# Agent attention with a top-1 expert layer: the last batch's first expert layer as one 128-row pass and a 19-row rest in four row groups

## The chip, the cores and the metric

The kernel runs on one core of a Trainium2 chip. The metric is the device time of one execution in microseconds (us), over several executions.

## What is computed

There are four batches of 11456 tokens, 128 channels, and 49 agents. Attention goes through the agents: `sm(agents, k)` weighs the values, `sm(q, agents)` weighs the result. Each token then goes through one of eight experts.

```
a2k = sm(agents, k);  agent_v = a2k @ v            # 49 x 128 per batch
x   = sm(q, agents) @ agent_v                      # 11456 x 128 per batch
e   = argmax(x @ w_gate);  g = max softmax(x @ w_gate)
out = g * (relu(x @ w1[e]) @ w2[e])                # w1: 128 x 1024, w2: 1024 x 128
```

## The kernel before

**Most tokens of a batch choose the same expert.** The kernel picks that expert for each batch (`choose`) and runs all tokens of the batch through it. Tokens that chose another expert are recomputed afterwards in blocks of 128 and their rows overwritten by an indirect scatter (`block_layer1` to `block_out`). There are 14 such blocks: 12 early ones from the first three batches, worked on during the last batch, and 2 late ones (numbers 12 and 13) from the last batch. A loop behind everything (`tc.For_i`, line 1681) would take any blocks beyond 14; here it makes no pass.

**First layer.** Since `x` is a product with `agent_v`, the first layer is computed from the 49 softmax values directly: the weights are `agent_v @ w1[e]`, 49 rows by 1024. All values are split into an upper and a lower fp16 part. The moving tile `M` holds the softmax numerators of a chunk of 1024 tokens, turned so that agents lie on partitions: the upper part in rows 0 to 48, the lower part in rows 64 to 112, zeros between. It is made in `mm` by `ehigh` and `elow` and turned by a DMA transpose (`eturn`, line 760). The stationary `Ah` holds the upper part of the weights, twice (rows 0 to 48 and 64 to 112), and `Al` the lower part likewise. So one eighth `f` of the 1024 hidden columns takes two matmuls over the same `M`, in `layer1`:

```python
nc.tensor.matmul(ph[:, :nn], st['Ah'][:, f, :], m, start=True, stop=False)
nc.tensor.matmul(ph[:, :nn], st['Al'][:, f, :], m, start=False, stop=True)
```

**A step** is one eighth of one group of 512 tokens: `layer1` (lines 1482, 1483; 512 columns each), `upper` on ScalarE (line 1489: relu to fp16), `lower` on VectorE (line 1494: the rest to fp16), `layer2` on TensorE (line 1507: 12 matmuls of 128 columns). A batch has 22 groups of 512 tokens and one of 192, 184 steps in all. `store` and `put` scale a finished group and write it.

**What sets the order.** `Plan` is a list scheduler with one queue per engine; each piece of work has a rank (its due step), a cost, what it needs and what it takes of the pools. Its order is then issued as it stands (`tc.manual_schedule`). Beside the steps of batch b stand the keys and values of batch b+1, the queries of the next chunks, the routing, and in the last batch the leftover blocks. Constants at the top (`BB`, `LL`, `QC3` and so on) shift the ranks.

**PSUM.** Of the eight banks `psH` has four (tag `h`, the first layer), `psY` two, `psS` two (`small_ps`). A bank of `psH` is free again when `lower` has read it.

## Time and profile before

| | us |
|---|---|
| three runs, median (lowest to highest) | 1068.8 (1067.12 to 1068.86) |
| the profiled execution, its own time | 1075.88 |
| its span, first to last instruction | 1074.2 |
| mean granted TensorE clock of it | 0.98 |
| TensorE matmul (PE) busy | 1021.5 (95%) |
| VectorE (DVE) busy | 905.9 (84%) |
| ScalarE (ACT) busy | 782.8 (73%) |
| GpSimd (POOL) busy | 168.9 (16%) |

Batches follow each other without a seam. The last batch's steps run from about 780 to 1053 us of the span, the last leftover blocks to 1062, and the end of the program to 1074.2. The ends of matmuls are modelled in the profile, so the distance between the starts of two matmuls says more than their durations. L12 is line 12 of the kernel before.

### The profile page before, as it was taken

The numbers are of one execution on the slowest core, as the hardware profiler recorded it, in microseconds if no ns is written. First come the engines' busy times: TensorE is split into PE (matmuls) and PEld (weight loads), VectorE is DVE, ScalarE is ACT, GpSimd is POOL, SyncE is SP. The second block draws the span as 40 slices with busy tenths as digits, with TensorE's granted clock in tenths as the row PEclk, the third lists the DMA queues.
The fourth block names the chain that finished last, engine by engine and source line by source line (L and its number), as shares of the span: only waits on it lengthen the run. The fifth ranks groups of instructions, "written<-read, shape, count | busy, mean of one in ns | idle before, by whom it ended". The sixth has DMA issues, their size and how long they took to land. (4 is left out here: it accounts for less than half of the span.)

```text
span 1074.2 us, 34781 instructions
## 1 busy us (share of the span) xinstructions
PE 1021.5 (95%) x14163; PEld 826.1 (77%) x14163; DVE 905.9 (84%) x2106; ACT 782.8 (73%) x1513; POOL 168.9 (16%) x390
## 2 busy tenths in 40 slices
PE   7979999999999999999999999999999799899995
PEld 6848878777887878777877887777877577688885
DVE  4888999978999899978999999868899878788651
ACT  6668888765788887765888887655876587567662
POOL 1000011003101111004012010004010423311210
PEclk8969999999999999999999999999999899999998
DMA  9778989992879979861989979852574486653320
GB/s 323 197 174 203 215 210 207 213 240 77 207 194 197 225 169 207 237 172 42 239 189 192 233 177 216 203 140 78 162 173 98 119 219 158 161 189 94 113 75 17
DMA packets 304324, 186.76 MB, mean 174 GB/s; under 512 B 217385, under 2 KB 275618, under 8 KB 304160
## 3 DMA queue, kind: packets, MB, share of 16 engines
q1 hardware_dynamic: 302304, 181.20, 68.3%
q0 software_dynamic: 1568, 2.25, 1.2%
q8 instruction: 112, 1.84, 0.7%
q10 hardware_dynamic: 288, 1.05, 0.3%
q14 instruction: 52, 0.43, 0.1%
HBM read 95.56 MB, written 36.43 MB: 123 GB/s over the span
## 5 line engine op out<-in xcount | busy, mean ns | idle before, releaser
L1507 PEld LDWEIGHTS <-hh 128*128 128x128 f16 x8640 | 536.5, 99 | 139.6 <-issue 13.2
L1507 PE MATMUL py<-w2h,hh 128*128 128x128 f16 (+1 forms) x5760 | 597.4, 219 | 2.8 <-issue 1.4
L1489 ACT ACTIVATE hh<-ph 128x512 f16<-128x512 f32 (+1 forms) x736 | 415.2, 588 | 202.4 <-PE ph L1483 190.4
L1494 DVE SCALAR_TENSOR_TENSOR hh<-ph,hh 128x512 f16<-128x512 f32 (+1 forms) x736 | 470.8, 667 | 71.1 <-ACT hh L1489 66.6
L1507 PE MATMUL py<-w2l,hh 128*128 128x128 f16 (+1 forms) x2880 | 519.6, 219 | 0.4 <-issue 0.3
L1482 PE MATMUL ph<-M,Ah 128*128 128x512 f16 (+1 forms) x736 | 276.3, 375 | 13.0 <-DVE hh L1494 12.6
L1483 PE MATMUL ph<-M,Al 128*128 128x512 f16 (+1 forms) x736 | 276.2, 375 | 0.5 <-DVE Al L898 0.3
L485 DVE SCALAR_TENSOR_TENSOR hl<-ld,mul,hl 128x1024 f16<-128x1024 f32 (+1 forms) x84 | 102.9, 1231 | 7.2 <-ACT hl L480 5.8
L472 POOL TENSOR_SCALAR mul<-hb 128x1 int32<-128x1 int32 (+1 forms) x90 | 27.4, 304 | 453.3 <-DVE hb L465 427.6
L480 ACT ACTIVATE hl<-ld,mul 128x1024 f16<-128x1024 f32 (+1 forms) x84 | 91.4, 1098 | 4.7 <-DMA ld<-in_q_dram 2.4
L446 ACT ACTIVATE jk<-ld 128x1024 f16<-128x1024 f32 (+1 forms) x90 | 90.7, 1008 | 4.4 <-DMA ld<-in_k_dram 2.8
L1483 PEld LDWEIGHTS <-Al 128*128 128x128 f16 x736 | 72.0, 98 | 24.8 <-issue 18.6
L1482 PEld LDWEIGHTS <-Ah 128*128 128x128 f16 x736 | 73.0, 99 | 10.2 <-issue 3.7
L755 POOL TENSOR_TENSOR mm<-E,mm 128x392 f16<-128x392 f32 (+1 forms) x30 | 28.6, 952 | 253.9 <-DVE mm L747 140.7
L541 PE MATMUL ps_small<-agh,hT 128*128 128x49 f16 (+1 forms) x630 | 58.2, 185 | 3.2 <-DMA hT<-hl 2.5
L543 PE MATMUL ps_small<-agh,hT 128*128 128x49 f16 (+1 forms) x630 | 58.2, 185 | 1.0 <-issue 1.0
L542 PE MATMUL ps_small<-agl,hT 128*128 128x49 f16 (+1 forms) x630 | 58.2, 185 | 0.5 <-issue 0.5
L541 PEld LDWEIGHTS <-hT 128*128 128x128 f16 (+1 forms) x630 | 52.0, 97 | 6.8 <-DMA hT<-hl 3.9
L1521 ACT ACTIVATE yo<-py,cs 128x128 f32<-128x128 f32 x174 | 49.8, 373 | 7.9 <-PE py L1507 7.2
L542 PEld LDWEIGHTS <-hT 128*128 128x128 f16 (+1 forms) x630 | 50.5, 97 | 3.4 <-issue 1.2
L543 PEld LDWEIGHTS <-hT 128*128 128x128 f16 (+1 forms) x630 | 50.3, 97 | 1.3 <-issue 1.3
L737 ACT ACTIVATE E<-E,ln,div 128x392 f32<-128x392 f32 (+1 forms) x48 | 33.0, 688 | 9.2 <-DVE E L732 8.9
(296 smaller groups left out, 1154.4 us busy)
## 6 DMA issues: line engine op xcount, KB each, us to landing
ld<-in_k_dram SPq DMA_DIRECT2D x44, 512.0 KB
ld<-in_v_dram SPq DMA_DIRECT2D x44, 512.0 KB
ld<-in_q_dram SPq DMA_DIRECT2D x44, 512.0 KB
out_dram<-yo SPq DMA_DIRECT2D x88, 256.0 KB
w1e<-in_moe_w_dram SPq DMA_DIRECT2D x17, 512.0 KB
w2e<-in_moe_w_dram SPq DMA_DIRECT2D x17, 512.0 KB
exps<-E SPq DMA_DIRECT2D x44, 196.0 KB
wn<-in_moe_w_dram SPq DMA_DIRECT2D x8, 512.0 KB
```

The lines of the kernel that those rows point to most:

```text
L446: nc.scalar.activation(jk[:p, :t * D], x[:p, :t, :].rearrange("p t d -> p (t d)"), AF.Square, accum_out=ss[:p])
L480: nc.scalar.activation(hl[:p, 0, :t, :], loaded[b, src, c][:p, :t, :], AF.Copy, scale=SC[src, c][0][:p, :1])
L485: nc.vector.scalar_tensor_tensor(hl[:p, 1, :t, :], loaded[b, src, c][:p, :t, :], SC[src, c][0][:p, :1], hl[:p, 0, :t, :], op0=ALU.mult, op ...
L541: nc.tensor.matmul(o, x[:, 0, i, :p], AG["h"], start=True, stop=False)
L542: nc.tensor.matmul(o, x[:, 0, i, :p], AG["l"], start=False, stop=False)
L543: nc.tensor.matmul(o, x[:, 1, i, :p], AG["h"], start=False, stop=True)
L1482: nc.tensor.matmul(ph[:, :nn], st['Ah'][:, f, :], m, start=True, stop=False)
L1483: nc.tensor.matmul(ph[:, :nn], st['Al'][:, f, :], m, start=False, stop=True)
L1489: nc.scalar.activation(hh[:, 0, :nn], ph[:, :nn], AF.Relu)
L1494: nc.vector.scalar_tensor_tensor(hh[:, 1, :nn], ph[:, :nn], 0.0, hh[:, 0, :nn], op0=ALU.max, op1=ALU.subtract)
L1507: mm_ = lambda l, r, **k: nc.tensor.matmul(o, l, r, skip_group_check=True, **k)
L1521: nc.scalar.activation(yo[:p, i, :], py[:p, i * D:(i + 1) * D], AF.Copy, scale=cs[:, i:i + 1])
```

## The change

It changes the last batch alone, and the end.

**Packing.** `mm` and `M` now use all 128 rows: the lower part in rows 0 to 48, the upper part in rows 66 to 114, and a second copy of the upper part for agents 0 to 16 in rows 49 to 65 and for agents 17 to 29 in rows 115 to 127 (`edup`, two casts on ScalarE per chunk). `Al` holds the upper weights for the first two parts and the lower weights for the copies (`packrow`, `restrow`). So one matmul with `Al` gives everything but the lower weights of agents 30 to 48, the leftover 19 rows.

**The rest.** `rests` computes those 19 rows for four eighths at once: four matmuls of 19 rows and 512 columns, at partitions 0, 32, 64 and 96 and into four different PSUM banks, three of `psH` and one of `psS`. Its moving rows lie in `M` at partitions 96 to 114 and are copied to the other three places by three DMAs per chunk (`rest`, tile `Q`, two buffers). `Wq` has the weights; `rest_products` makes them with four small fp32 matmuls per batch, `rest_split` splits them.

**The end.** `block_out` of blocks 12 and 13 stands behind the loop in the source and leaves the plan. `keep`, the pool with their indices and values, outlives the main pools.

Beside that: the gathered rows `ex` are transposed without the copy `ex2` (line 1286); `BB` is 86 in place of 80 (the leftover blocks' rank); eleven small VectorE operations at the start make `packrow` and `restrow`. The built order of batches 0 to 2 is the same up to the preparation of the last batch's weights.

```diff
+KR = 128 - 2 * A
+UP = 96 - KR
+DUP = ((A, 0, UP - A), (UP + A, UP - A, KR))
-BB, BS, BLAG, BZ, WL, WS = 80, 8, 3, 3, 22, 10
+BB, BS, BLAG, BZ, WL, WS = 86, 8, 3, 3, 22, 10
...
+        def edup(c):
+            _, p, t = chunks[c]
+            for o, a0, a1 in DUP:
+                nc.scalar.copy(mm[c % len(mm)][:p, :t, o:o + a1 - a0], Es[c][:p, :t, a0:a1])
+
+        def rest(c):
+            _, p, t = chunks[c]
+            x = Qs[c] = mpool.tile([P, 8, P], F16, tag="Q", name="Q", bufs=MQ)
+            for r in range(3):
+                nc.sync.dma_start(x[32 * r:32 * r + A - KR, :t, :p], Ms[c][96:96 + A - KR, :t, :p])
...
+        def rest_products():
+            st["Wq"] = one.tile([P, 2, P], F16, tag="mx", name="Wq")
+            pq = AV["aq"] = small_ps()
+            w1q = AV["w1"].rearrange("d (p s r) -> d r s p", s=2, r=4)
+            for r in range(4):
+                nc.tensor.matmul(pq[32 * r:32 * r + 32, :2 * P], AV["avq"][:, r, :], w1q[:, r], start=True, stop=True)
...
+        def rests(g, s_):
+            c, h, n = groups[g]
+            nn = n * chunks[c][1]
+            for r in range(4):
+                k_ = slice(32 * r, 32 * r + A - KR)
+                ph = hs[g, 4 * s_ + r] = small_ps() if r == 3 else psH.tile([P, 512], F32, tag="h", name="ph")
+                nc.tensor.matmul(ph[:, :nn], st['Wq'][k_, s_, :], st['Q' if r < 3 else 'M'][c][k_, h:h + n, :chunks[c][1]],
+                                 start=True, stop=False)
+
         def layer1(g, f):
             c, h, n = groups[g]
             nn = n * chunks[c][1]
+            if packed:
+                ph = hs[g, f]
+                nc.tensor.matmul(ph[:, :nn], st['Al'][:, f, :], st['M'][c][:, h:h + n, :chunks[c][1]], start=False, stop=True)
+                hs[g, f] = ph, nn
+                return
...
+                if packed and f % 4 == 0:
+                    add(("R", i), i - 0.05, "PE", 0.1 + 0.32 * u, rests, g, f // 4, r=[(b, "rest", c), (b, "wq2"), (b, "eturn", c), ("L1", i - 1)],
+                        take=[bank(i + x) for x in range(4)], free=[("Q", (b, "q", c))] if f == 4 and (g + 1 == NG or groups[g + 1][0] != c) else [])
...
-        add(("bo", u), t + BLAG + 6, "POOL", 1.2, block_out, u, r=[("bs", u)] + ([(B - 1, "put", g) for g in range(NG)] if late else []), land=1.5, move=0.2)
+        if not late:
+            add(("bo", u), t + BLAG + 6, "POOL", 1.2, block_out, u, r=[("bs", u)], land=1.5, move=0.2)
...
+    for u in range(NSE, NS):
+        block_out(u)
```

On TensorE, in the last batch, a step of the kernel before reads as follows (ph is the first layer's bank, hh its fp16 halves, py the second layer's bank; ten more rows of line 1507 follow).

```order
L1482 LDWEIGHTS Ah_16028
L1482 MATMUL ph_16453<-M_15899,Ah_16028 128x512
L1483 LDWEIGHTS Al_16029
L1483 MATMUL ph_16453<-M_15899,Al_16029 128x512
L1507 LDWEIGHTS hh_16363
L1507 MATMUL py_16373<-w2h_16070,hh_16363 128x128
```

With the change, four steps begin with the rest in four banks, each of which then gets its one pass (left out are the weight loads of Wq).

```order
L1551 LDWEIGHTS Wq_16165
L1551 MATMUL ph_16688<-Q_16428,Wq_16165 128x512
...
L1551 MATMUL ph_16690<-Q_16428,Wq_16165 128x512
...
L1551 MATMUL ph_16692<-Q_16428,Wq_16165 128x512
...
L1551 MATMUL ps_small_16694<-M_16342,Wq_16165 128x512
L1559 LDWEIGHTS Al_15963
L1559 MATMUL ph_16688<-M_16342,Al_15963 128x512
```

Line 1482 is gone, and the first matmul into the three banks of `psH` (tile `ph`) and the one of `psS` (`ps_small`) is now issued before any of the four passes.

On VectorE, late in the last batch, the kernel before has these rows between the steps' `lower` (yb is a leftover block's output, wsp a leftover block's split weights):

```order
L1494 SCALAR_TENSOR_TENSOR hh<-ph,hh 128x512 x4
L1344 SCALAR_TENSOR_TENSOR wsp<-w1e,tsm_17263,wsp 128x1024
L1494 SCALAR_TENSOR_TENSOR hh<-ph,hh 128x512
L1375 TENSOR_SCALAR yb<-pyb,fgt 128x128
L1494 SCALAR_TENSOR_TENSOR hh<-ph,hh 128x512 x6
```

With the change the same kinds of rows stand there:

```order
L1410 SCALAR_TENSOR_TENSOR wsp<-w1e,tsm_17308,wsp 128x1024
L1576 SCALAR_TENSOR_TENSOR hh<-ph,hh 128x512 x2
L1576 SCALAR_TENSOR_TENSOR hh<-ps_small,hh 128x512
L1576 SCALAR_TENSOR_TENSOR hh<-ph,hh 128x512 x2
L1410 SCALAR_TENSOR_TENSOR wsp<-w1e,tsm_17308,wsp 128x1024
L1576 SCALAR_TENSOR_TENSOR hh<-ph,hh 128x512
```

Every fourth `lower` reads a bank of `psS`, and a long split still stands between two steps.

On GpSimd at the end, the kernel before has (out with 45824 rows is a late block's scatter, ntot the loop's count, lines 1681 and 1769 the loop):

```order
L1385 DMA out_dram<-yb,fti 45824x128
L1680 TENSOR_LOAD ntot
L1681 COMPARE_AND_BRANCH
...
L1681 UNCONDITIONAL_BRANCH
L1385 DMA out_dram<-yb,fti 45824x128
L1714 UNCONDITIONAL_BRANCH
```

and with the change:

```order
L1451 DMA out_dram<-yb,fti 45824x128
L1768 TENSOR_LOAD ntot
L1769 COMPARE_AND_BRANCH
...
L1769 UNCONDITIONAL_BRANCH
L1451 DMA out_dram<-yb,fti 45824x128
L1806 UNCONDITIONAL_BRANCH
```

In both, one late scatter is issued ahead of the loop and one behind it.

## Rows read from the trace of the kernel before

**Rows 1.** Busy time by stretch of the last batch, and of two earlier stretches.
```profile
core 0: us, PE busy (x) PEld busy (x) DVE busy (x) ACT busy (x) POOL busy (x), PEclk, DMA share, GB/s
0.00:60.00 60.00, 47.45 (x554) 44.40 (x554) 39.01 (x126) 39.16 (x72) 6.66 (x45) 0.90 0.85 255
120.00:180.00 60.00, 59.50 (x920) 47.79 (x917) 57.89 (x107) 52.40 (x96) 7.63 (x18) 1.00 0.95 210
780.00:840.00 60.00, 59.29 (x827) 46.21 (x826) 55.30 (x131) 44.23 (x87) 10.66 (x17) 1.00 0.61 146
840.00:860.00 20.00, 13.76 (x166) 10.32 (x164) 18.05 (x50) 11.38 (x24) 7.61 (x10) 0.83 0.41 83
860.00:1000.00 140.00, 131.77 (x1703) 110.47 (x1701) 113.44 (x304) 97.11 (x216) 38.49 (x36) 1.00 0.58 161
1000.00:1058.00 58.00, 58.00 (x756) 51.31 (x756) 32.57 (x61) 37.96 (x82) 7.03 (x6) 1.00 0.26 83
```
**Rows 2.** The same stretches, matmuls of line 1482 alone; columns PE, PEld, clock, DMA.
```profile
780.00:840.00 60.00, 19.30 (x51) 4.97 (x51) 1.00 0.61 146
840.00:860.00 20.00, 3.86 (x9) 0.94 (x9) 0.83 0.41 83
860.00:1000.00 140.00, 31.53 (x84) 8.51 (x84) 1.00 0.58 161
1000.00:1058.00 58.00, 13.62 (x39) 3.72 (x38) 1.00 0.26 83
```
**Rows 3.** Timeline of PE, one step: start us, us, what.
```profile
1044.31 0.38 PE L1482 MATMUL ph<-M,Ah 128*128 128x512 f16 x1
1044.52 0.38 PE L1483 MATMUL ph<-M,Al 128*128 128x512 f16 x1
1044.74 0.22 PE L1507 MATMUL py<-w2h,hh 128*128 128x128 f16 x1
...
1045.41 0.38 PE L1482 MATMUL ph<-M,Ah 128*128 128x512 f16 x1
```
**Rows 4.** Who PE waited for from 780 us on; its two longest waits, timeline.
```profile
PE ph L1482 <- DVE hh L1494: 7.6, 6, 2.6
```
```profile
843.22 0.38 PE L1482 MATMUL ph<-M,Ah 128*128 128x512 f16 x1 [1.90 <-DVE hh L1494]
...
852.59 0.58 PE L1482 MATMUL ph<-M,Ah 128*128 128x512 f16 x1 [2.62 <-DVE hh L1494]
...
854.68 0.63 PE L1482 MATMUL ph<-M,Ah 128*128 128x512 f16 x1
```
**Rows 5.** Timeline of PE and PEld: values, fp32 pairs in two column halves, between fp16 work.
```profile
221.19 0.22 PE L1507 MATMUL py<-w2h,hh 128*128 128x128 f16 x1
221.34 1.86 PE L629 MATMUL ps_small<-ld,S 128*64 128x129 f32 x30
...
223.25 0.39 PE L1482 MATMUL ph<-M,Ah 128*128 128x512 f16 x1
...
223.24 0.10 PEld L1482 LDWEIGHTS <-Ah 128*128 128x128 f16 x1 [0.17 <-issue]
```
**Rows 6.** Timeline of PE: fp32 matmuls of 128 columns that use the whole array.
```profile
1059.83 2.01 PE L1370 MATMUL pyb<-w2e,hb 128*128 128x128 f32 x16
```
**Rows 7.** Timeline of PE: scores, a weight load and 49 columns each, 24 in all.
```profile
805.48 0.19 PE L541 MATMUL ps_small<-agh,hT 128*128 128x49 f16 x1
...
806.08 0.38 PE L1482 MATMUL ph<-M,Ah 128*128 128x512 f16 x1
```
**Rows 8.** Groups by form, DVE and ACT, 780 to 1058 us: busy us, mean ns.
```profile
L1494 DVE SCALAR_TENSOR_TENSOR hh<-ph,hh 128x512 f16<-128x512 f32 x176 | 115.1, 682 | 29.1 <-ACT hh L1489 27.2 <-issue 1.7
L1344 DVE SCALAR_TENSOR_TENSOR wsp<-w1e,tsm,wsp 128x1024 f16<-128x1024 f32 x14 | 18.1, 1301 | 2.2 <-ACT wsp L1341 2.1
L485 DVE SCALAR_TENSOR_TENSOR hl<-ld,mul,hl 128x1024 f16<-128x1024 f32 x9 | 12.2, 1355 | 0.1
L1489 ACT ACTIVATE hh<-ph 128x512 f16<-128x512 f32 x176 | 101.6, 602 | 56.9 <-PE ph L1483 49.6 <-PE ph L1355 2.7 <-issue 2.6
L1521 ACT ACTIVATE yo<-py,cs 128x128 f32<-128x128 f32 x88 | 25.2, 372 | 6.8 <-PE py L1507 6.6
```
**Rows 9.** Instructions of one line: the products of the first layer's weights (ns min/median/max), and a one-column VectorE operation.
```profile
L888 PE MATMUL ps_small<-w1e,av x12: 592/592/648, 293.8 to 771.8; 128*128 128x512 f32 x12
```
```profile
L465 DVE TENSOR_SCALAR hb<-ss 128x1 int32<-128x1 int32 x77 | 9.6, 143 | 2.1 <-ACT jk L446 2.1
```
**Rows 10.** The end: timeline of SP, DVE and POOL, then the chain that ended last.
```profile
1059.00 0.33 SPq L1528 DMA_DIRECT2D out_dram<-yo  x1
1059.31 0.35 DVE L1375 TENSOR_SCALAR yb<-pyb,fgt 128x128 f32<-128x128 f32 x1 [5.04 <-PE pyb L1370]
1061.56 0.98 POOL L1385 DMA_INDIRECT out_dram<-yb,fti  x1 [15.72 <-SPq L1681]
1061.88 0.35 DVE L1375 TENSOR_SCALAR yb<-pyb,fgt 128x128 f32<-128x128 f32 x1 [2.23 <-PE pyb L1370]
1068.86 0.98 POOL L1385 DMA_INDIRECT out_dram<-yb,fti  x1 [6.31 <-issue]
```
```profile
1061.56 4.69 DMA out_dram<-yb,fti
```

More of the change, by code (lines that the diff above doesn't have):

```diff
@@ L652, in agentvalues @@
                 AV["avt"] = wpool.tile([P, 2, 64], F32, tag="av", name="av")
-                nc.vector.memset(AV["avt"], 0.0)
+                if not last:
+                    nc.vector.memset(AV["avt"], 0.0)
             elif i == 3:
@@ L881, in weights_scale @@
             nc.vector.tensor_scalar(AV["d1"].bitcast(I32), hb, AV["pb"], None, op0=ALU.add)
+            if last:
+                AV["rm"] = two.tile([P, 1], F32, tag="rm", name="rm")
+                nc.vector.tensor_tensor(AV["rm"], AV["m1"], restrow, op=ALU.mult)
         def first_products(j):
@@ L895, in first_split @@
             if up:
-                nc.scalar.activation(st["Ah"][:, :, o], x, AF.Copy, scale=m)
+                nc.scalar.activation(st["Ah"][:, :, o], x, AF.Copy, scale=AV["rm"] if last else m)
             else:
@@ L1028, in attention @@
                 (1, "PE", 0.25, [n_("vsum", NCK - 1)], ["e"], [("acc", n_())]), (3, "PE", 0.25, [n_("vsum", NCK - 1)], ["v"], [("acc", n_())]), (2, "DVE", 0.75, [av(1)], [], ["e"]),
-                (4, "DVE", 0.5, [av(2), av(3)], [], ["v"]))):
+                (4, "DVE", 0.9 if last else 0.5, [av(2), av(3)], [], ["v"])) + (((13, "POOL", 0.6, [av(4)], [], []),) if last else ())):
             add(av(i), base + te + 0.02 * m, g, w, agentvalues, i, r=r, take=[("s", n_("av", x)) for x in tk_],
@@ L1057, in attention @@
             add(n_("fl", j), o + 0.05, "DVE", 0.68, first_split, j, False, r=[n_("fu", j)], free=[(small, n_("fp", j))])
+        if last:
+            o = base + tw + 1 + 4 * WSP
+            add(n_("fq"), o - 0.5, "PE", 1.0, rest_products, r=[n_("wload"), av(13), n_("wx", 1), n_("fp", 1)], take=[("s", n_("fq"))], free=[("ld", n_("w1"))])
+            add(n_("uq"), o, "ACT", 0.45, rest_split, True, r=[n_("wx", 1), n_("fq")])
+            add(n_("wq2"), o + 0.05, "DVE", 0.4, rest_split, False, r=[n_("uq")], free=[("s", n_("fq"))])
         add(n_("su"), base + tw + 1.3 + 3 * WSP, "ACT", 1.05, second_split, True, r=[n_("wx", 2)])
@@ L1079, in attention @@
                     (eturn, 10, "SP", 1.3, None, dict(take=[("M", n_("q", c))], free=[(m_, n_("q", c))], land=LANDM, move=1.5))):
-                add(n_(f.__name__, c), base + t + d[e], g, w, f, c, r=r or [prev], **kw)
+                if f is edup and not last:
+                    continue
+                if f in (elow, edup):
+                    r = [n_("ehigh", c)]
+                if f is eturn and last:
+                    r = [n_("elow", c), n_("edup", c)]
+                add(n_(f.__name__, c), base + t + (d[e] if e % 1 == 0 else 0.7 * d[8] + 0.3 * d[9]), g, w, f, c, r=r or [prev], **kw)
                 prev = n_(f.__name__, c)
+            if last:
+                add(n_("rest", c), base + t + d[10] + RD, "SP", 1.1, rest, c, r=[n_("eturn", c)], take=[("Q", n_("q", c))], land=2.0, move=0.3)
             add(n_("estore", c), base + t + d[10] + 2, "SP", 0.4, estore, c, r=[n_("qexp", c)], free=[("S", n_("q", c))], land=1.2, move=0.6)
@@ L1283, in prepare_blocks @@
         yield
-        ex2 = one.tile([P, UG, A], F32, tag="fx2", name="fx2")
-        nc.scalar.copy(cut(ex2), cut(ex))
-        yield
         ae = ldp.tile([P, 2, UG, P], F32, tag="ld", name="fae")
@@ L1294, in prepare_blocks @@
         for i in range(n):
-            nc.tensor.transpose(ps[:A, i * P:(i + 1) * P], ex2[:, i, :], ident)
+            nc.tensor.transpose(ps[:A, i * P:(i + 1) * P], ex[:, i, :], ident)
         yield
@@ L1373, in block_store @@
         _, gt, ti = blocks[u]
-        yo = bh[u, "yo"] = two.tile([P, D], F32, tag="yb", name="yb")
+        yo = bh[u, "yo"] = (two if where[u][2] else keep).tile([P, D], F32, tag="yb", name="yb")
         nc.vector.tensor_scalar(yo, bh.pop(u)[:, :D], gt, None, op0=ALU.mult)
@@ L1635, in agent_moe_kernel @@
                 r += [(B - 1, "estore", c) for c in range(NCK)]
-            if i == 10 and not early:
+            if i == 9 and not early:
                 r.append((B - 1, "av", 11))
```

72 lines of the change are left out of this document (52 added, 20 removed).

## The prediction, before the result was known

> **What bounds the kernel now.** I read the busy shares by stretch first, then one step on TensorE, then what TensorE waited for, then the end.
>
> The reader is to see in the stretches that the last batch is not one thing [rows 1]. From 1000 to 1058 us TensorE (PE) is busy for 58.0 of 58 us and VectorE (DVE) for 32.6: there every column that TensorE no longer streams is time. From 860 to 1000 us PE has 131.8 of 140 and DVE 113.4, still room. From 780 to 840 us both are full, 59.3 and 55.3 of 60. From 840 to 860 us PE has only 13.8 of 20 and DVE 18.1: there DVE sets the pace.
>
> One step takes 1.10 us [rows 3]: the two passes start 0.21 and 0.22 us apart, 0.43 together, and the twelve matmuls of the second layer fill the other 0.67. That is TensorE streaming without a hole.
>
> PE's waits for DVE's `lower` to free a bank make 7.6 us, six times, from 780 us on [rows 4]. After the longest, 2.62 us, two steps lie 2.09 us apart, and the granted clock of the 20 us around it is 0.83 [rows 1, 4]; full steps being 1.10 us, PE then ran at the lower of its two levels (1.2 GHz), and came back to 2.4.
>
> **The first layer's passes.** Four steps have eight passes of 0.215 us, 1.72 us. With the change they have four, 0.86, and one rest. Of the rest no row shows the thing itself, four row groups; I bound it by the nearest.
>
> - Do parts of the array work side by side? The values' matmuls are fp32 of 129 columns in two column halves: 30 are recorded in the 1.91 us from their first start to the next fp16 pass, 0.064 us each [rows 5]. fp32 of 128 columns over the whole array takes 2.01/16 = 0.126 each [rows 6]. So two halves do overlap almost fully. I take the same for four row groups.
> - How far apart do the four start? Scores have a weight load and 49 columns each, 24 of them in 0.60 us, 0.025 apart [rows 7]. Three such distances make 0.075.
> - What does going over cost? Into the halves: the last fp16 matmul starts at 221.19, and with twelve matmuls in 0.67 us its successor would have started at 221.25; the first of the halves starts at 221.34, so 0.09. Out again: the weight load of line 1482, else hidden, comes only at 223.24, 0.17 us after the load before it, and I put that at 0.10 [rows 5].
>
> A rest then takes 0.09 + 0.215 + 0.075 + 0.10 = 0.48 us. The ends are 0.22 (all four at once, nothing for going over) and 1.05 (four passes one behind another, and going over). Four steps save 0.86 - 0.48 = 0.38 us, a step 0.095. There are 44 such fours: 16.7 us. The group of 192 columns has passes of 0.215 x 192/512 = 0.08 us: four of them, 0.32, against a rest of 0.09 + 0.08 + 0.075 + 0.10 = 0.35. It saves nothing.
>
> **What of it is on the path.** Per stretch, with the steps counted by line 1482 [rows 2]:
> - 780 to 840: 51 steps could save 4.9 us, but DVE's 55.3 us do not shrink. Its best share in a stretch of steps is 57.89 of 60, 0.965 [rows 1], so at least 57.3 us are needed: 2.7 us.
> - 840 to 860: DVE-bound; nothing.
> - 860 to 1000: 84 steps, 8.0 us; DVE's floor of 113.4/0.965 = 117.6 is not reached.
> - 1000 to 1058: 39 steps, eight of them short, so 31: 3.0 us.
>
> Together 13.7 us. That the rank of the leftover blocks moves (`BB`) shifts DVE work from the first stretch to the later ones, which would let the first save more; I count it in a rival.
>
> **A new wait: the banks.** Before, a step needs one of the four `psH` banks, the one that `lower` of four steps earlier has freed: 4 x 1.10 - 0.43 = 3.97 us after that step's pass, and `upper` and `lower` need 0.60 + 0.68 and some 0.2 for the handing over [rows 3, 8], so 2.5 us are to spare. With the change a rest takes three of four at once, so the second step of the four before must be through. Its pass ends 0.91 us after its own rest began (0.48 + 2 x 0.215); the next rest is due at 0.48 + 0.86 + 4 x 0.67 = 4.02. In these 3.1 us lie one `upper`, two `lower` and the handing over, 2.1: only 1.0 us to spare. The 23 long splits of DVE in the batch, 1.30 us and 1.36 [rows 8], overrun that by 0.3: between 0 (all fall elsewhere) and 7 us. I take 4, somewhat over half.
>
> **The small parts.**
> - `edup`: 24 casts on ScalarE of 136 and 104 columns; the nearest row is 0.372 us for 128 [rows 8], 9 us, less the copies of `ex2`. ScalarE has 190 of 278 us in these stretches: hidden. Its cover would be gone if it went over DVE's share.
> - `rest_products`: eight fp32 instructions of 256 columns, half of the 0.592 us of 512 [rows 9]: 2.4 us one behind another, 0.6 if the four column parts overlap. I take 1.0, on PE, ahead of the batch.
> - `rest`: 36 DMAs on SP. What stands behind them there are leftover weights and outputs; the next rest waits for them. DMA is at 0.26 to 0.61 busy after 780 us, against 0.95 before [rows 1]. Nothing, up to one bank wait of 2.6 us [rows 4].
> - Eleven one-column operations at the start, 0.143 us each [rows 9], 1.6 at most; DVE is busy for 39 of the first 60 us [rows 1], yet some stand in the agents' chain. 0.3.
> - The end: nothing. The built order has one late scatter ahead of the loop and one behind it, before and after. The first is held not by its own block, ready at 1059.66, but by the outputs' DMAs, the last of them issued at 1059.00; it starts at 1061.56, its landing takes 4.69, the loop's exit follows it, and the second starts at 1068.86 [rows 10].
>
> **The sum.** -13.7 + 4 + 1.0 + 0.3 = -8.4 us against the profiled execution, 1075.9 to 1067.5. That execution lies 7.1 us above the median of the three runs, outside their range; I take the difference over unchanged: 1068.8 - 8.4 = **1060.4 us**.
>
> **The rivals.**
>
> *TensorE stays the bound throughout.* With leftover work moved back, no DVE floor in the first stretch and no bank waits: -16.7 + 1.3 = -15.4, and if the two longest stops (2.62 and 1.90 us, [rows 4]) go too, -20: 1053 to 1049. For it: DVE has 219 us of work in 278. Against it: its shares in the first 80 us. By the Trainium skill, "TensorE: Matmul & The Clock Gate", section on packing small matmuls, four row groups of 32 rows and 512 columns were measured at 3.07 times the speed of one behind another. By that the rest takes 4 x 0.215/3.07 = 0.28 us, my 0.215 + 0.075 without going over, the fours save 0.58 us, and this rival would end near 1045; no run here shows it.
>
> *The banks take it back.* Every long split costs its 0.3 us, 7 us, and three more stops like that of 2.62 us send the clock to its lower level. Steps at 2.09 us lose 1 us each, two to four of them a stop: 9 us. -13.7 + 7 + 9 + 1.3 = +3.6: 1072. It ends on the other side once waits and clock pass 12.4 us, 0.28 us per rest. For it: the longest stop came from just this wait [rows 4]. Against it: six such waits in 183 steps so far. The Trainium skill, "TensorEngine Tiling (Array Packing)", section on the PSUM bottleneck, says that after a faster TensorE the copying out of PSUM may bind; the first stretches [rows 1] agree, the later ones don't.
>
> *The row groups run one behind another.* Then a rest is 0.86 + 0.19 = 1.05 us, the fours lose 0.19 us each, 8.4 us, of which the DVE-bound 60 steps hide some 2.7: +7 with the small parts, **1076, slower**. It decides from a rest of 0.86 us. For it: no row of four row groups. Against it: the two halves overlapped.
>
> *The end does what the source says.* If both scatters went behind the loop, the 4.69 us of the first landing would come after the exit, and the two would overlap: up to 5 us less. The built order speaks against it.
>
> **How the numbers follow.** A measurement of this kernel can tell some 0.2%, 2.1 us, from no change. Forecast (1056 to 1065) 0.45; TensorE throughout (1045 to 1055) 0.25; banks (1065 to 1074) 0.17; one behind another 0.10; the rest, the end among it, 0.03. Faster by over 2.1 us: the first two, two fifths of the banks, nearly nothing of the last: 0.77. Within: 0.07. Slower: 0.16. The range 1048 to 1071 leaves out the last but one case, the worst of the banks and the best of the second, 0.2.
>
> **What would show it.** The four matmuls of a rest start under 0.1 us apart and the next pass some 0.45 to 0.5 us after the first: right; over 0.8: one behind another. From 1000 us on, four steps take about 4.0 us in place of 4.4. PE's waits for `lower` grow from 7.6 us to between 10 and 20, most of them ahead of a rest. From the last matmul (1059.83 + 2.01, [rows 6]) to the end of the span it stays 12.4 us. Steps of over 2 us beside a low clock, or a PE share under 0.85 in the stretch after 860 us, would make me wrong.

## The result, and the profile after

The changed kernel takes 1081.6 us (median of four runs, 1076.7 to 1082.8), the kernel before beside it 1068.8 (four runs, 1067.1 to 1070.8). The ratio is 1.0119, with a 95% interval of 1.0095 to 1.0142: slower by 12.8 us, where 8.4 us faster was forecast. The profiled execution of the change is a typical one, 1082.2 us (span 1080.3). That of before, 1075.9, is not, so the profiles lie 6.1 us apart and not 12.8; what is read from them below is kept within the last batch.

Busy time by stretch after the change, in the columns of [rows 1]:

```profile
780.00:840.00 60.00, 51.71 (x787) 40.72 (x785) 55.27 (x139) 39.94 (x92) 8.10 (x13) 1.00 0.63 144
840.00:860.00 20.00, 15.99 (x230) 12.01 (x228) 15.94 (x41) 12.84 (x29) 7.44 (x9) 1.00 0.48 97
860.00:1000.00 140.00, 126.63 (x1690) 105.79 (x1688) 117.79 (x308) 100.55 (x231) 37.37 (x40) 0.96 0.61 156
1000.00:1058.00 58.00, 56.16 (x735) 48.60 (x733) 35.97 (x72) 35.77 (x77) 9.45 (x9) 0.97 0.34 112
```

PE is busy for less in each of the long stretches, and the clock, 1.00 in [rows 1] from 860 us on, is now 0.96 and 0.97. DVE in the first 60 us is where it was: 55.27 after, 55.30 before.

The timeline of PE at one rest, between the second layer of one step and the next pass:

```profile
1030.33 0.22 PE L1589 MATMUL py<-w2h,hh 128*128 128x128 f16 x1
1030.48 0.39 PE L1551 MATMUL ph<-Q,Wq 19*128 19x512 f16 x3
1030.49 0.39 PE L1551 MATMUL ps_small<-M,Wq 19*128 19x512 f16 x1
1030.81 0.82 PE L1559 MATMUL ph<-M,Al 128*128 128x512 f16 x3
```

The four row groups start within 0.01 us of each other, and the next pass comes 0.33 us later. Ahead of the rest lie 0.15 us where 0.055 are usual between these matmuls, so going over costs 0.095. Going out again is inside the 0.33: the next pass comes 0.317 us after the fourth start, where two passes lie 0.215 apart, so 0.10 more. A rest is 0.43 us in all. The saving in columns is there.

Who PE waited for from 780 us on, after the change:

```profile
PE py L1589 <- DVE hh L1576: 11.3, 11, 2.6
PE ph L1551 <- DVE hh L1576: 5.1, 6, 1.4
PE pyb L1436 <- DVE yb L1441: 2.7, 2, 1.9
PE ps_small L804 <- DMA M<-mm: 2.4, 2, 1.6
PE ps_small L804 <- DVE tei L1244: 2.2, 1, 2.2
PE py L1589 <- ACT hh L1571: 1.5, 1, 1.5
```

Line 1551 is the rest: it waits for banks 5.1 us, less than the passes did before (7.6, [rows 4]). New are the waits of line 1589, the second layer, for `lower` of its own step, 11.3 us, and of line 804, the logits, for the transposes of M and for DVE.

Summed over the timeline of PE from the batch's first first-layer matmul to the last matmul (holes over 0.12 us counted as waits): before, 282.7 us (779.10 to 1061.84), 14.8 of them waits; after, 282.2 (785.98 to 1068.16), 27.2 of them waits. **In these two executions the batch has the same length: 13 us less work, 12.4 us more waiting.** In second profiles of both it is 284.5 us, 15.1 of them waits, and 287.0, 29.5 of them waits.

These two marks do not enclose quite the same work, since more of batch 2's second layer stands ahead of the first rest than stood ahead of the first pass before. A mark with the same steps behind it in both kernels is the first pass of batch 2's short group (192 columns). From there to the last matmul it is 289.0 us before and 289.4 after; in the second profiles 290.7 and 294.0.

Both profiles of before hold a stop in the last batch. In the first one VectorE and ScalarE stand together for 5.4 us from 913 us on, and TensorE goes on in pieces, with waits that the profile puts down to nothing (timeline of DVE and ACT):

```profile
918.53 0.57 DVE L731 TENSOR_REDUCE mq<-ps_small 128x8 f32<-128x392 f32 x1 [5.82 <-PE ph L1483]
918.62 0.60 ACT L1489 ACTIVATE hh<-ph 128x512 f16<-128x512 f32 x1 [5.45 <-PE ph L1483]
```

In the second profile it is 5.6 us at 915. Neither profile of the change has such a stop in the last batch, nor have the four kernels below that keep the order of before in this place (half `lower` and the three with passes left out). Without it, by estimate, before would be some 5.5 us shorter and the change 6 to 9 us longer in this stretch, which is of the size of the loss that the runs show. What causes the stop no row says. The mark itself lies between 767.9 and 780.5 us over the profiles of all kernels below, whose order up to there is nearly the same; so no profile tells what part of the loss lies ahead of it.

### The profile page after: what moved, and what is told of

It is laid out like the page before. It is cut to its first block, busy times and chain, and to the rows that moved or that the text cites. A ratio compares the mean times of both kernels' runs of the same rounds, so it can differ in the third digit from the quotient of the medians.

```text
span 1080.3 us, 34844 instructions
## 1 busy us (share of the span) xinstructions
PE 1012.7 (94%) x14171; PEld 817.8 (76%) x14171; DVE 909.0 (84%) x2119; ACT 780.6 (72%) x1534; POOL 168.4 (16%) x392
## 5 line engine op out<-in xcount | busy, mean ns | idle before, releaser
L1589 PE MATMUL py<-w2h,hh 128*128 128x128 f16 (+1 forms) x5760 | 592.4, 220 | 15.3 <-DVE hh L1576 11.3
L1571 ACT ACTIVATE hh<-ph 128x512 f16<-128x512 f32 (+1 forms) x690 | 384.9, 588 | 196.7 <-PE ph L1565 142.1
L1576 DVE SCALAR_TENSOR_TENSOR hh<-ph,hh 128x512 f16<-128x512 f32 (+1 forms) x690 | 440.7, 668 | 68.9 <-ACT hh L1571 66.0
L1564 PE MATMUL ph<-M,Ah 128*128 128x512 f16 (+1 forms) x552 | 207.7, 376 | 5.2 <-DVE hh L1576 5.0
L1565 PE MATMUL ph<-M,Al 128*128 128x512 f16 (+1 forms) x552 | 207.6, 376 | 0.5 <-DVE Al L953 0.5
L458 ACT ACTIVATE jk<-ld 128x1024 f16<-128x1024 f32 (+1 forms) x90 | 90.7, 1008 | 10.4 <-DMA ld<-in_q_dram 7.7
L484 POOL TENSOR_SCALAR mul<-hb 128x1 int32<-128x1 int32 (+1 forms) x90 | 27.2, 303 | 441.0 <-DVE hb L477 392.5
L1565 PEld LDWEIGHTS <-Al 128*128 128x128 f16 x552 | 54.2, 98 | 12.4 <-issue 8.9
L1564 PEld LDWEIGHTS <-Ah 128*128 128x128 f16 x552 | 55.0, 100 | 7.8 <-issue 4.6
L761 ACT ACTIVATE E<-E,ln,div 128x392 f32<-128x392 f32 (+1 forms) x48 | 33.1, 689 | 11.5 <-DVE E L756 11.3
```

What stands on the lines that cost most here:

```text
L458: nc.scalar.activation(jk[:p, :t * D], x[:p, :t, :].rearrange("p t d -> p (t d)"), AF.Square, accum_out=ss[:p])
L1571: nc.scalar.activation(hh[:, 0, :nn], ph[:, :nn], AF.Relu)
L1576: nc.vector.scalar_tensor_tensor(hh[:, 1, :nn], ph[:, :nn], 0.0, hh[:, 0, :nn], op0=ALU.max, op1=ALU.subtract)
L1589: mm_ = lambda l, r, **k: nc.tensor.matmul(o, l, r, skip_group_check=True, **k)
```

## The experiments

The kernel before has medians of 1066.5 to 1077.4 us from one group of runs to the next. Times below are compared only with the runs of before that were made beside them, as a ratio with its 95% interval.

**A second look at before** (no edit).

> The kernel before, unchanged, for a second profile. Its first profiled execution lay 7 us above its other runs, so the 6.1 us between the two profiles are not the 12.8 us between the medians. Theory A (the packed passes turn saved columns into waits of TensorE in the last batch): a profile near 1069 us, in which the last batch, from its first first-layer pass to the last matmul, is 7 us shorter than the 282.7 us of the first profile, and batches 0 to 2 end at 779 us as they did. Theory B (the batches ahead are what the change made slower): the last batch stays at 282 to 283 us and batches 0 to 2 end 6 to 7 us earlier than 779.

Measured: 1079.6 us in its one execution, 1077.4 the median of before beside it; from the second split of the weights (775.36 us here, 773.59 in the first profile) to the last matmul 290.0 us against 288.3. Neither theory's number came: the second profile repeats the first, with the stop at 915. It was made beside runs of 1077.4 us, so it can't tell how a run of 1068.8 us spends its time; the stop of 5.4 us is the nearest to the 7 us by which the first profile lay over its runs.

**The small parts alone.**

```
-BB, BS, BLAG, BZ, WL, WS = 80, 8, 3, 3, 22, 10
+BB, BS, BLAG, BZ, WL, WS = 86, 8, 3, 3, 22, 10
...
-    keep = pl("keep", 2)
...
-        ex2 = one.tile([P, UG, A], F32, tag="fx2", name="fx2")
-        nc.scalar.copy(cut(ex2), cut(ex))
...
+    for u in range(NSE, NS):
+        block_out(u)
```

> The kernel before with the change's other parts alone: keep's place in memory and the late scatter behind the loop, the transposes reading ex without the copy ex2, BB 86 in place of 80; no rest, no packed passes, no constants for them. Theory A: 1066 to 1071 us, no change that can be told. Theory B (these parts or the memory's layout slow the batches ahead or the leftover blocks): 1075 to 1082 us.

Measured: 1.0014 (0.9985 to 1.0043). The other parts cost nothing that can be told, with 0.4% as the upper end. Theory B falls for them; the loss is, at least for the most part, in the packed first layer and what feeds it.

**The passes spread, and BB back.**

```
-LL, RG, RD, L1S, MQ = 5, 0.7, 2, 0.5, 2
+LL, RG, RD, L1S, MQ = 5, 0.7, 2, 1.0, 2
```

> The changed kernel with the four passes behind a rest due one step apart (L1S 1.0) and not half a step. If the bunching of the passes is what makes layer2 wait for lower (theory A1): upper and lower get their work at an even pace, layer2's 11.3 us of waits fall under 5, 1072 to 1077 us. If the banks are (theory A2: a rest can start only when lower has freed three of four): the waits move to the rests and the time stays within 3 us of 1081.6. Theory B: unchanged, within 2 us.

Measured: 1.0098 (1.0067 to 1.0129), 1087.6 us. Layer2 still waits 12.5 us for `lower`; bunching is not the cause. Nor did the waits move to the rests, as theory A2 had it: those for `lower` are 2.1 us.

> The changed kernel with BB back at 80. Theory A: the leftover blocks' DVE work goes back six steps earlier; within 3 us of 1081.6 either way. If the moved rank is what costs (it puts long splits beside the packed steps): 1070 to 1076 us.

Measured: 1.0145 (1.0095 to 1.0196), 1094.7 us. The moved rank is not what costs: taking it back gains nothing. Whether it loses, against a change at 1.0054 to 1.0119 in other groups of runs, is not shown.

**The change again.**

> The changed kernel once more, timed beside the kernel before on the chip of the next three. Theory A (TensorE's streaming falls by some 13 to 16 us and its waits in the last batch rise by 12, so that from the second split of the batch's weights to the last matmul it takes 3 to 4 us longer than before's 288 to 290): ratio 1.003 to 1.007, the rest of the 1.012 being scatter of the batches ahead. Theory B (the batches ahead really run slower, by their memory layout or constants): ratio 1.010 to 1.014 again.

Measured: 1.0054 (1.0021 to 1.0086), the ratio of theory A; but in its profile it is 296.9 us from the second split to the last matmul, 7 to 9 us more than in the two of before and not 3 to 4. Against 1.0119 in the first pairing the size is uncertain by a factor of two; the sign is not. The granted clock, a mean over the whole execution, was 0.9769 over its ten runs and 0.9796 over the 19 of before: (1 - clock) x time is 25.0 us against 22.0, so up to 3.1 of the 6.0 us between the means can be TensorE's clock.

**Rests of two.** In the order as built, layer2 of a step stands two steps or fewer behind that step's first layer in 3 of 184 cases before and in 21 after; five steps behind in 146 and 53. The planner holds a rest until four banks are free and lets PE run the second layer in the meantime, so that it catches up with `lower`.

```
+        width = lambda g: 2
...
+                rw = width(g)
...
-                if packed and f % 4 == 0:
+                if packed and f % rw == 0:
...
-                        take=[bank(i + x) for x in range(4)], ...
+                        take=[bank(i + x) for x in range(rw)], ...
```

> A rest for two steps, in two row groups, in place of four: all of its banks are psH, two at once, and none of psS. First layer: 2 x 0.215 and a rest of 0.43, 0.86 us for two steps, as before the change: no column is saved. Theory A2 (that a rest claims four banks at once is what lets layer2 catch up with lower in the planned order: in the packed order 21 of 184 steps have their layer2 two or fewer steps behind the first layer, before 3, here 5): layer2's waits for lower fall from 11.3 us to under 5, and the time is within 0.4% of the kernel before, 0.995 to 1.004. Theory C (DVE's other work stands in other places since BB moved, and layer2 would wait in any case): layer2's waits stay over 8 us and the ratio over 1.010.

Measured: 1.0211 (1.0169 to 1.0253). Half of theory A2 came: the waits for `lower` fell to 3.5 us. The time rose all the same. The waits of PE in this kernel:

```profile
PE ps_small L804 <- DMA M<-mm: 7.6, 4, 2.2
PE ph L1553 <- DVE hh L1578: 3.5, 5, 2.8
PE py L1591 <- DVE hh L1578: 3.5, 2, 2.8
```

The logits now wait 7.6 us for M, and the first layer, entries into the rests counted, streams some 3 us more than before the change. What the rest of the 20 us is, these rows don't say.

> Rests of two steps in the first eight groups (64 steps, where DVE sets the pace) and of four from the ninth on. Theory A2: in 30 fours the first layer saves 0.43 us each, 13 us, of which waits take back some 5: 0.988 to 0.996 of the kernel before. If four banks at once cost as much in the later stretch as they save: 1.002 to 1.008.

Measured (`rw` is 2 in the first eight groups, 4 from there): 1.0163 (1.0108 to 1.0218). Outside both expectations; waits for M are 10.8 us. A2 as the whole story falls.

**Layer2 not waiting.**

```
-                mm_(x[:, 1, s], st['w2h'][:, f, :], start=False, stop=(f == FT - 1))
+                mm_(x[:, 0 if packed else 1, s], st['w2h'][:, f, :], start=False, stop=(f == FT - 1))
```

> The changed kernel, in the last batch with the third matmul of each part of the second layer reading the upper half hh[:, 0] again in place of the lower half, so that layer2 no longer waits for lower; the low half's share of the products is left out. lower itself runs as it did, and a rest still waits for it to free its banks. Theory A3 (the waits cost what they show): the 11.3 us go, the time falls by 8 to 12 us against the changed kernel, to 1068 to 1073 where that takes 1081. Theory A2 strict (the banks are the true limit and the wait only moves): rests wait over 12 us in place of 5.6, and the time falls by under 4 us.

Measured: 1.0051 (1.0018 to 1.0084); the change beside it had 1.0054. Taking the largest wait away gave nothing: PE's waits in the batch still sum to 29.8 us, against 27.2 and 29.5 in the two profiles of the change. Its longest waits now:

```profile
PE ph L1551 <- DVE hh L1576: 9.3, 12, 1.7
PE ps_small L804 <- DMA M<-mm: 5.9, 4, 2.5
PE py L1589 <- issue: 3.3, 6, 1.1
PE pyb L1436 <- DVE yb L1441: 2.7, 2, 1.9
PE py L1589 <- ACT hh L1571: 2.3, 2, 1.7
PE ps_small L1551 <- DVE hh L1576: 1.6, 2, 0.8
```

The same `lower` is now waited for by the rests, 9.3 + 1.6 us in place of 5.6. A wait that moves when it is taken away was a symptom: PE is held to the pace of `lower`, at one place or the other.

**DVE relieved, in both kernels.**

```
+            nl = nn // 2 if b + 1 == B else nn
-            nc.vector.scalar_tensor_tensor(hh[:, 1, :nn], ph[:, :nn], 0.0, hh[:, 0, :nn],
+            nc.vector.scalar_tensor_tensor(hh[:, 1, :nl], ph[:, :nl], 0.0, hh[:, 0, :nl],
...
-                mm_(x[:, 1, s], ...
+                mm_(x[:, 0 if b + 1 == B and 2 * i >= n else 1, s], ...
```

> The kernel before, in the last batch with lower over the first half of the columns alone (the second layer's low part of the other half reads the upper half again; that share of the products is left out). DVE is relieved of some 0.3 us a step, 50 us in 184 steps, and banks come free sooner. TensorE's 15 us of waits go at most: 0.987 to 0.997 of the kernel before.

Measured: 0.9993 (0.9968 to 1.0019), above the range expected. Busy time from 780 to 840 us:

```profile
780.00:840.00 60.00, 59.39 (x845) 47.28 (x844) 44.36 (x130) 46.36 (x92) 10.28 (x17) 1.00 0.64 150
```

DVE has 11 us less to do than in [rows 1], and line 1482 starts 51 steps, as many as before: here TensorE itself is full.

> The changed kernel with the same half lower. Theory D (the saved columns are there, but lower on DVE and the banks that it frees set the pace, so they turn into waits): with DVE relieved the saving shows, 11 to 16 us below the kernel before with half lower, 0.974 to 0.985. Theory F (the work that feeds the packed passes holds it back: the copies of edup on ScalarE ahead of the transposes, the loads of rest on SP's queue): DVE's relief helps both alike, and it ends within 4 us of the kernel before with half lower.

Measured: 1.0029 (1.0003 to 1.0055), 5 us above before with the same relief. Theory D alone falls, and theory F's 4 us are missed by one. PE waits now first for M:

```profile
PE ps_small L804 <- DMA M<-mm: 8.2, 3, 3.5
PE py L1590 <- DVE hh L1577: 5.9, 7, 2.4
PE ph L1551 <- DVE hh L1577: 2.8, 3, 1.3
```

**The feeding left out.** What stands ahead of M is seen on SP's queue in the changed kernel:

```profile
891.91 4.95 SPq L505 DMA_TRANSPOSE hT<-hl  x1
896.95 1.94 SPq L778 DMA_DIRECT2D Q<-M  x3
899.00 2.22 SPq L797 DMA_TRANSPOSE M<-mm  x1
```

Three loads of Q hold the queue for 1.94 us, and M's transpose goes out behind them; at 907.29 the logits wait 1.57 us for an M.

```
-            for o, a0, a1 in DUP:
+            for o, a0, a1 in ():
...
+            if c:
+                Qs[c] = Qs[0]
+                return
             x = Qs[c] = mpool.tile([P, 8, P], F16, tag="Q", name="Q", bufs=MQ)
```

> The changed kernel without the feeding: edup's 24 copies are left out (the rests multiply what the tiles held) and Q is loaded for the first chunk alone, 3 loads in place of 36, all later rests reading that. All passes, rests and banks as in the changed kernel. Theory F: M's transposes go out as early as before, logits no longer wait for M (4.7 us before, nearly 0 here), and the time falls by 10 us or more, to 0.985 to 0.996 of the kernel before. Theory D: it falls by under 4 us, 1.001 to 1.006.

Measured: 1.0048 (1.0027 to 1.0068). The waits for M are gone from the trace, and the time hardly moves. What PE waits for instead:

```profile
PE py L1592 <- DVE hh L1579: 10.4, 12, 3.0
PE ph L1554 <- DVE hh L1579: 3.1, 5, 1.3
```

> The changed kernel without edup's copies alone, with all 36 loads of Q. Theory F, if ScalarE's copies are the half that costs: as the one without any feeding, within 3 us. If the loads on SP are: as the changed kernel, 1.003 to 1.008. Theory D: 1.001 to 1.008.

Measured: 1.0071 (1.0048 to 1.0093). The copies alone cost nothing that can be told; they were hidden on ScalarE.

**Both taken away.**

> The changed kernel with half lower and without the feeding, both at once (left out: half of the low part of the second layer, edup's copies, 33 of 36 loads of Q). Theory G (two limits side by side, lower with its banks and the late transposes; each hides the other's relief): TensorE's waits in the last batch fall under 14 us and the saved columns show, 0.983 to 0.992 of the kernel before. Theory H (neither is the limit; the saving is lost to TensorE's own clock or to work that no wait shows): 0.998 or more.

Measured: 0.9936 (0.9908 to 0.9964), 6 us below before with half `lower` (0.9993). Set against the change's 1.0054, the two reliefs by themselves are 0.3% (1.0029) and 0.1% (1.0048), and both together 1.2%: more than their sum, as theory G has it with two limits side by side, though short of its 0.992. Theory H falls. But each ratio has some 0.3% of interval either way, and against the first pairing's 1.0119 the two alone would already make 1.6 of 1.8%, so that they hide each other is not shown by the ratios. The profiles point to it: from the mark at batch 2's short group to the first rest of the ninth group it is 93.0 and 95.5 us in the change, 91.0 with half `lower`, 90.8 without the feeding, and 84.1 with both. The waits of PE for M are gone, those of layer2 for `lower` are 8.2 us.

**Are columns time at all?**

```
...
-            nc.tensor.matmul(ph[:, :nn], st['Al'][:, f, :], m, start=False, stop=True)
+            if b + 1 < B:
+                nc.tensor.matmul(ph[:, :nn], st['Al'][:, f, :], m, start=False, stop=True)
```

> The kernel before, in the last batch without the second first-layer pass (line 1483 left out there, so half of the first layer's products are missing): 184 passes, 39 us of TensorE, less, and nothing else touched. If columns on TensorE are time in the last batch, as the prediction took for 2/3 of them: 0.970 to 0.982 (20 to 32 us). If TensorE only seems full and its neighbours set the pace: 0.990 or more (under 11 us), and the gaps grow by what the passes save.

Measured: 0.9916 (0.9899 to 0.9934), 1057.2 us against 1066.5. Of some 39 us of passes left out, 9 us came off: **a quarter**. The kernel has the order of before, its banks and its feeding, so nothing of the change can be blamed. PE's waits and three stretches of this kernel:

```profile
PE ph L1482 <- DVE hh L1495: 16.4, 15, 4.5
PE ph L1353 <- DVE hh L1495: 2.6, 4, 1.2
```

```profile
780.00:840.00 60.00, 51.20 (x796) 42.81 (x795) 55.36 (x133) 43.79 (x88) 10.80 (x17) 1.00 0.64 148
840.00:860.00 20.00, 14.15 (x167) 11.97 (x167) 19.16 (x51) 12.17 (x27) 8.98 (x11) 0.74 0.39 82
860.00:1000.00 140.00, 128.51 (x1761) 114.30 (x1759) 121.64 (x321) 105.24 (x233) 40.62 (x39) 0.98 0.64 169
```

From 780 to 840 us PE's busy time falls from 59.3 to 51.2 us and DVE's stays at 55.4, and line 1482 starts 52 steps, before 51: the passes became idle time of PE, not progress. Its waits for `lower` grow from 7.6 to 16.4 us, and the clock falls further than in [rows 1].

**The loads of Q elsewhere.**

```
-                nc.sync.dma_start(x[32 * r:32 * r + A - KR, :t, :p], ...
+                nc.gpsimd.dma_start(x[32 * r:32 * r + A - KR, :t, :p], ...
...
-                add(n_("rest", c), base + t + d[10] + RD, "SP", 1.1, rest, c, ...
+                add(n_("rest", c), base + t + d[10] + RD, "POOL", 3.0, rest, c, ...
```

> The changed kernel with the 36 loads of Q issued by POOL in place of SP. In the changed kernel three of them hold SP's queue for 1.94 us ahead of a transpose of M. Theory F2 (SP's queue makes M late): logits' waits for M go from 2.3 to 4.7 us to under 1, and the time falls by 3 to 5 us. If POOL, whose gathers then come later, hands it on: 0 to 5 us slower than the changed kernel.

Measured: 1.0174 (1.0149 to 1.02). The logits' waits for M are gone; one wait of a leftover block for `lower`, 5.5 us, stands among new ones, and from the last matmul to the end of the span it is 16.5 us, where the other profiles have 12.1 to 12.6.

> The changed kernel with the loads of Q due 6 steps after M's transpose in place of 2 and planned at 2.0 us in place of 1.1, so that the next transposes go out ahead of them on SP. Theory F2: 1.002 to 1.006. If rests then wait for Q: 1.008 or more.

Measured (RD 6 in place of 2, planned at 2.0 us): 1.0152 (1.0114 to 1.0191). Layer2 waits 14.0 us for `lower`, and the times of both are no better than the change's. Moving the loads does not mend it.

**Where columns are time.** The edit is that of one pass, under `g < 8` and under `g >= 15`.

> The kernel before, in the last batch's first eight groups (64 steps) with one first-layer pass in place of two (the second pass's share of the products is left out): 13.8 us less for TensorE, there where DVE's share is 0.9 and more. Theory J (columns are time only where DVE leaves room): under 4 us, 0.996 to 1.001. If columns are time there as elsewhere: 0.987 to 0.991.

Measured: 0.9985 (0.9964 to 1.0006), 1.6 us of 13.8.

> The same in the last eight groups (from the sixteenth on; seven of 512 columns, one of 192): 56 x 0.215 and 8 x 0.08, 12.7 us less for TensorE. Theory J: 7 to 11 us, 0.990 to 0.994. If the saving is lost there too, to the clock or to the leftover blocks: 0.996 or more.

Measured: 0.9920 (0.9891 to 0.9949), 8.5 us of 12.7. Theory J holds at both ends. The waits of PE, first with the early passes gone, then with the late ones gone:

```profile
PE ph L1482 <- DVE hh L1495: 15.7, 14, 4.5
```

```profile
PE ph L1482 <- DVE hh L1495: 7.5, 3, 4.6
```

and the stretches, early passes gone:

```profile
780.00:840.00 60.00, 49.56 (x776) 41.50 (x775) 55.30 (x137) 44.97 (x92) 9.88 (x16) 0.98 0.64 141
```

late passes gone:

```profile
1000.00:1040.00 40.00, 40.00 (x569) 37.78 (x567) 22.80 (x44) 27.88 (x64) 3.92 (x3) 1.00 0.24 84
```

The early passes turn into waits, DVE standing at 55.30 us once more, and into a lower clock: by the mean clocks of the runs (0.9802 against 0.9837) TensorE loses 3.7 us more to it than before. With the late ones gone PE stays full to the last slice.

Between the two lie seven groups that neither run touched. From the first pass of the ninth group to that of the sixteenth it is 89.9 and 89.7 us in these two profiles, and 88.6 with all second passes left out: 1.2 us of 12.0, a tenth. So columns are time in the last eight groups and hardly before them.

## Why the prediction was wrong, step by step

**The price of the rest: right.** Forecast 0.48 us, measured 0.33 + 0.095 = 0.43. Going in (0.09) and out (0.10) came as forecast; the four starts are 0.01 us apart in all and not 0.075. (In [rows 5] 32 matmuls of the values lie in the 1.91 us, 0.060 each, where the prediction counted 30; nothing hangs on it.) Row groups run side by side, and the rival in which they run one behind another is out. The first layer of the batch, streamed, went from 79.8 us to 41.3 for the passes, 18.4 for the rests and 44 x 0.095 = 4.2 for going over: 15.9 us less, where 16.7 were forecast.

**What of it is on the path: the step that failed.** The prediction put 13.7 of 16.7 us on the path, four fifths. The runs put it at a quarter for the batch as a whole (9.3 of 38.5), an eighth in the first eight groups (1.6 of 13.8), a tenth in the seven behind them (1.2 of 12.0, by profiles) and two thirds in the last eight (8.5 of 12.7). By a quarter, the most that this change could bring was some 4 us, by estimate. Two choices in that step were wrong. For 780 to 840 us it allowed DVE to rise to 0.965, its best share in a stretch of batches 0 to 2 [rows 1]; but DVE stood at 55.3 of 60, 0.92, before, after, and with the passes left out: no share above that came in this stretch, with its in-order queue of short operations and gathers. DVE is not alone in that: with DVE at 44.36 us (half `lower`) the stretch moved as little, TensorE being full. Two engines bind there side by side. For 860 to 1000 us, its largest term (8.0 of 13.7), it counted every saved column because DVE had 19% idle; up to the sixteenth group, near 950 us, a tenth was measured. An engine that serves a chain of steps, one `upper` and one `lower` behind each, can bind long before its share is full; with 39 us of passes gone DVE reached 121.6 of 140, 0.87, and PE waited.

**The banks: the wait came in another place, and larger.** Forecast +4 us, between 0 and 7, ahead of rests. PE's waits grew by 12.4 us (14.8 to 27.2; 15.1 to 29.5 in the second profiles), and the rests' part is smaller than the passes' was. The working gave the slack of a bank and not that of layer2 behind `lower`, which the built order shows to be thinner (21 steps against 3). How a DVE queue then holds PE is plain in one place of the changed kernel, timeline of DVE, then of PE:

```profile
845.51 0.16 DVE L1325 TENSOR_TENSOR fr<-tsl,fg 128x4 f32<-128x4 f32 x1 [2.84 <-DMA fg<-ranks,fri]
845.71 0.53 DVE L1326 TENSOR_TENSOR fm<-fg,fr 128x360 f32<-128x360 f32 x1
846.27 0.53 DVE L1327 TENSOR_REDUCE fr<-fm 128x4 f32<-128x360 f32 x1
846.72 0.68 DVE L1576 SCALAR_TENSOR_TENSOR hh<-ps_small,hh 128x512 f16<-128x512 f32 x1
```

```profile
847.46 0.23 PE L1589 MATMUL py<-w2h,hh 128*128 128x128 f16 x1 [1.93 <-DVE hh L1576]
```

DVE waits 2.84 us for a gather of a leftover block, this operation and two more follow, and only then the `lower` that layer2 of its step needs. Before, DVE stood for the same gather, and with layer2 mostly five steps behind PE came to a stop at a pass instead, 1.90 us at 843.22 [rows 4]:

```profile
839.12 0.17 DVE L1256 TENSOR_TENSOR fr<-tsl,fg 128x4 f32<-128x4 f32 x1 [2.19 <-DMA fg<-ranks,fri]
```

So the thin cover moves such a stop and is not the cause by itself: with layer2's wait removed, PE's waits in the batch were as long as with it.

**The loads of Q on SP: costed at nothing, wrong.** "Nothing, up to one bank wait" looked at who stands behind them on paper; M's transposes do too. The logits wait 2.4 and 4.7 us for M in two profiles of the change, 0 in both profiles of before from 780 us on. Even so the time without the loads is much the same; only beside half `lower` does leaving the feeding out show (1.0029 to 0.9936).

**The clock: in a rival, not in the forecast.** Slices of the changed kernel, after stops of PE:

```profile
880.00:900.00 20.00, 15.16 (x207) 11.44 (x205) 18.29 (x47) 15.12 (x33) 6.11 (x8) 0.83 0.98 256
960.00:980.00 20.00, 18.06 (x215) 15.72 (x213) 16.76 (x52) 14.72 (x34) 1.80 (x2) 0.91 0.55 180
1000.00:1020.00 20.00, 18.16 (x213) 14.64 (x211) 12.64 (x31) 10.41 (x22) 5.45 (x5) 0.91 0.39 113
```

Their missing shares are 0.17, 0.09 and 0.09 of 20 us, 7.0 us, against 3.4 in the one low slice of before [rows 1]. PE stood still for 2.59 us at 888, 1.94 at 968 and 1.41 at 1008 ahead of them, and ran at 1.2 GHz, the lower level, for parts of what followed. But the second profile of before loses as much as the first of the change:

```profile
840.00:860.00 20.00, 13.85 (x167) 10.28 (x165) 17.14 (x50) 11.21 (x24) 6.38 (x11) 0.83 0.41 84
900.00:920.00 20.00, 17.04 (x223) 14.10 (x221) 12.51 (x28) 12.06 (x31) 9.32 (x11) 0.98 0.65 151
920.00:940.00 20.00, 18.41 (x201) 15.29 (x201) 15.84 (x44) 11.89 (x24) 4.93 (x5) 0.85 0.49 149
```

These make 6.8 us, and the second profile of the change loses 8.5 in the batch. So one profile doesn't give the size; the mean clocks of 10 and 19 runs do, and by them some 3 us more than before go to the clock (25.0 against 22.0), half of the 6.0 us between the means. Where the feeding is left out it is 6.8 us more (0.9764 against 0.9827), more than the 4.8 by which that kernel is slower. Whether the stops bring the clock down is read from the slices alone; no run parts the two. So 15.9 us of columns saved meet 12.4 to 14.4 us more of waits, some 3 us of clock and 1.1 us of `rest_products`, and nothing is left.

**Small steps.** `rest_products` 1.1 us for a forecast 1.0:

```profile
777.68 1.11 PE L936 MATMUL ps_small<-w1e,avq 128*32 128x256 f32 x8
```

`edup` hidden: right (24 casts, 0.30 us in the median; without them nothing is gained). The end: right.

```profile
1065.63 0.35 DVE L1441 TENSOR_SCALAR yb<-pyb,fgt 128x128 f32<-128x128 f32 x1 [4.79 <-PE pyb L1436]
1068.20 0.35 DVE L1441 TENSOR_SCALAR yb<-pyb,fgt 128x128 f32<-128x128 f32 x1 [2.22 <-PE pyb L1436]
```

```profile
1067.94 0.97 POOL L1451 DMA_INDIRECT out_dram<-yb,fti  x1 [10.19 <-SPq L1769]
1074.99 0.97 POOL L1451 DMA_INDIRECT out_dram<-yb,fti  x1 [6.08 <-issue]
```

One scatter still starts ahead of the loop's exit and one behind it, as in [rows 10]; from the last matmul's end to that of the span it is 12.1 us, before 12.4.

**The rivals.** Nearest came "the banks take it back", waits of 7 us and a clock of 9, 1072 us, slower than before by 3.6. Its two mechanisms are those that were seen, waits behind DVE and the clock, with other sizes (12.4 and some 3) and not at the banks alone. "TensorE stays the bound throughout" is what the one-pass runs refute. A rest does the work of 4 x 0.215 us in 0.33, 2.6 times as fast, and 2.0 times with going over. The Trainium skill, "TensorE: Matmul & The Clock Gate", section on packing small matmuls, has 3.07 for four row groups of 32 rows and 512 columns; the trace, with 19 rows, agrees in kind and stays below it, the more so with the going over. The Trainium skill, "TensorEngine Tiling (Array Packing)", section on the PSUM bottleneck, says that the copying out of PSUM may bind once packing makes TensorE faster; the one-pass runs, which relieve TensorE without packing, agree (16.4 us of waits for `lower`, 9 of 39 us gained).

**What stays open.** Why the loss is 1.2% in one pairing and 0.5% in another, and how much of it lies ahead of the last batch; what the stop in the profiles of before is; what of the time of the rests of two lies behind their waits. A version with rests of four in the last groups alone, where two thirds of a column are time, was not tried: 14 fours there would spare 14 x 0.43 = 6 us of columns, by the measured share some 4 us. The change itself has those fours, and no such gain shows in it: from the first layer of the sixteenth group to the last matmul it is 104.6 and 101.7 us in its two profiles, 102.0 and 101.9 before. PE's waits there grew from 1.4 and 1.3 us to 4.6 and 4.5, and 16 matmuls more of the leftover blocks, 2.0 us, stand there since `BB` moved.

## What to carry to other kernels

Before costing a saving on an engine that looks full, take the same work away outright (leave a pass out, in one stretch at a time) and see what the time does: here that put the worth of a column at an eighth in one stretch and at two thirds in another, where the busy shares of PE, 0.99 and 1.00, looked the same. The best share of a second engine elsewhere is not the share that it reaches in that very stretch; where both are near full, relieving either alone showed nothing here. And a wait that is removed and comes back under another name is the pace of the engine waited for: look for the limits that lie side by side, and relieve two at once before giving up on either.

## What was not expected of the hardware

The time of an execution goes with the granted clock of TensorE, a mean over the span: among the runs of the change beside one another, 1075.9 us at 0.981, 1082.1 at 0.978 and 1087.1 at 0.975, nearly 2 us a thousandth; a line through the ten runs gives 1.3. With 39 us of passes left out the mean clock fell to 0.976 (before beside it 0.9825), so (1 - clock) x time rose from 18.7 to 25.4 us: 6.7 us of what was left out went back that way, beside the 9 that came off. And half `lower`, 41 us less of DVE in the last batch (178.5 against 219.7 us of its busy time from 780 to 1060 us), moved the kernel before by nothing that can be told, though PE's longest waits were for that very instruction: PE was busy for 59.39 of the first 60 us all the same.
